# Column 0 of two folds on another engine, gathers ahead of angle rows, ten products moved into the last tiles, and transform copies put off

## The chip, the cores and the metric

The kernel runs on one core of one Trainium2 chip. A core has five engines that the text speaks of by their profile names: PE (TensorE, matrix products; its weight loads are PEld), DVE (VectorE), ACT (ScalarE), POOL (GpSimd) and SP (SyncE, which here only issues transfers). Each engine works through its own queue in order, and the engines wait for one another through semaphores, which are counters: an instruction names a counter and the value that it must have reached. The metric is the device time of one execution in microseconds (us); lower is better.

## The reference, cut to what matters

```python
X = np.fft.fft(x, axis=1)            # x: 8 batches x 3008 rows x 256 channels
X = np.fft.fft(X, axis=2)
x = X.real.reshape(8 * 3008, 256)
gate = np.maximum(x @ w_gate, 0.0)   # 256 -> 1536
val = x @ w_val
out = (gate * val) @ w_out           # 1536 -> 256, float32
```

So each batch gets a two-dimensional Fourier transform, of which the real part goes through a gated layer: two products with weight matrices, the relu of one times the other, and a third product.

## The kernel before, in words

**The transform.** The transform over the 256 channels is taken into the weights: TA and TB are cosine and sine matrices, and the kernel forms WA (cosine times weight) and WB (sine times weight) for gate and value. What is left is the transform over the 3008 rows. By symmetry it is folded: a row is added to, or subtracted from, its mirror row, in two halves of the batch (r = 0, 1) and three tiles of 128 row pairs (t = 0, 1, 2). XD holds rows read upward, XG the mirror rows read downward. Their sum goes to AA, and from AA the cosine inputs F and the sine inputs G are formed, 128 channels each. Products of F and G with tables of cosines and sines (`tabC`, `tabS`) then give the transform, U and V, whose columns are output rows.

**The start (batch 0).** For row tile 0 the mirror rows are loaded upward and turned by a product with a reversed identity (`turn`, L347). For row tiles 1 and 2 GpSimd issues four indirect gathers (`load_mirror`, L118), between small row fills: `iota` (L224) writes the index and angle rows, among them `urow`, of which two columns per row tile feed the angle products (`angle`, L313 and L314) that make the odd tables on ScalarE. After that GpSimd issues the first weight loads (`load_w`, L295), finishes TA and TB (L361, L363), and issues the other four weight loads and that of `w_out` (L367). On VectorE a loop over t folds: for t = 0 and each half, L422 writes channels 1 to 255 of AA, L423 channel 0 (which is stored twice, at 0 and at 256), then F (L391 for half 0, L389 for half 1), a small difference `hy` for channel 128 (L397), and G (L405). For t = 1 and 2 one L411 writes channels 1 to 255 of both halves, L412 channel 0, and then come F for both halves, `hy` and G for both halves. ScalarE turns `hy` into `ny` (L401). `dft_first` takes the products (L575, in the loop order half, then parity of the row pair) into four banks, with the weight products (L589) and angle products of later tables between them; ScalarE copies one bank out (L545, `es`), and VectorE forms sum and difference (L555) into U and V.

**The tiles.** The output is worked in blocks of columns, and each block in 12 tiles of 128 of the 1536 inner features. Batch 0 has four blocks of 376 or 377 columns, the others three blocks of 512, 512 and 481. A tile of batch 0 (`single_tile`) has on TensorE the gate (L816, L817), the mirror of the tile before (L822), the value (L816, L817) and the mirror of the gate (L822); ScalarE takes the relu (L832), and VectorE the product h (L841) for the column and its mirror. In later batches (`slot`) the gate is split over ScalarE, VectorE (L967) and GpSimd (L968), and VectorE forms h twice in a tile (L852). The output products with `w_out` (L729) of the block before are spread between these, some per tile; 24 of them, two groups of 12, fill a bank, which ScalarE copies (L742) and SP sends out (L752).

**The transform of the next batch** is a list of steps (`dft_steps`, L538) that batch 0 takes after its tiles, as many as the table `DFT_0` says. When a bank is complete, `end` puts its copy (L545, list `evict`) and its sums (L555, list `sums`) on two lists; in batch 0 `flush` issues both at once, and `run`, which a tile calls for output products, flushes too. The channel-128 rows are made in one step of this list (`nyquist_steps`), with two copies (L663).

**The end.** In the last block 8 output products per tile are taken (96 in 12 tiles). When the last tile's mirror and h are done, the block's own 96 output products follow without other work. SP moves the h columns that do not fill a group of 128 rows to a buffer LB (L847), which the last-but-one group reads.

The order on each queue is that in which the Python code issues the instructions; the tile framework adds the waits between engines from what each instruction reads and writes.

Of the kernel before, what the change touches and what calls it, by code (L numbers as in the profile page):

```python
# [15 lines left out]
ALU = mybir.AluOpType  # L16
# [18 lines left out]
def kernel(  # L35
# [8 lines left out]
    nc = tc.nc  # L44
    B, S, D = x.shape
# [177 lines left out]
    def iota(dst, pattern, base, mult):  # L223
        nc.gpsimd.iota(dst, pattern=pattern, base=base, channel_multiplier=mult, allow_small_or_imprecise_dtypes=True)  # L224
# [60 lines left out]
    iota(back[:], [[0, 1]], 127, -1)  # L285
    iota(gidx[:].rearrange("p (t r) -> p t r", r=2), [[-128, 3], [-H // 2, 2]], H - 1, -1)
    load_mirror(0, 1, 0)
    for t in (1, 2):
        iota(urow[0:1, 2 * t:2 * t + 2], [[1, 2], [2, 128]], 256 * t + 1, 0)
    nc.gpsimd.memset(urow[0:1, 5, 120:121], 0.0)  # L290
    load_mirror(0, 1, 1)
    hold(slice(2, 3))

    def load_w(i, c):
        nc.gpsimd.dma_start(out=wr[i][c], in_=(moe_w_gate, moe_w_val)[i][:, c * 512:(c + 1) * 512].rearrange("(c p) f -> p c f", p=128))  # L295
    for r in range(2):
        load_mirror(0, 2, r)
    load_w(0, 0)
    load_w(1, 0)
    nc.gpsimd.memset(sgn[:], 1.0)  # L300
# [60 lines left out]
    nc.gpsimd.tensor_scalar(TB[:, 0, 0:1], ad[:, 128:129], scalar1=-1.0 / 128, op0=ALU.mult, scalar2=0.5, op1=ALU.add)  # L361
    for T in (TA, TB):
        nc.gpsimd.tensor_tensor(T[:, 1, :], T[:, 0, :], sgn[:], op=ALU.mult)  # L363
    for c in (1, 2):
        for i in range(2):
            load_w(i, c)
    nc.gpsimd.dma_start(out=wo[:], in_=moe_w_out.rearrange("(c p) d -> p c d", p=128))  # L367
# [39 lines left out]
    for t in range(3):  # L407
        n = ROWS[1][t]
        p = slice(0, n)
        if t:  # L410
            nc.vector.tensor_tensor(AA[p, :, t, :, 1:D], XG[p, :, t, ::-1, 1:D], XD[p, :, t, :, D - 1:0:-1], op=ALU.add)  # L411
            nc.vector.tensor_tensor(AA[p, :, t, :, 0:D + 1:D], XG[p, :, t, ::-1, 0].unsqueeze(3).to_broadcast([n, 2, 2, 2]),  # L412
                                    XD[p, :, t, :, 0].unsqueeze(3).to_broadcast([n, 2, 2, 2]), op=ALU.add)
            for r in range(2):
                channels(p, r, t)
            half_128(p, t)
            for r in range(2):
                channels_g(p, r, t)
        else:
            nc.vector.memset(GG[1][:].rearrange("p i t q d -> p (i t q) d")[:, :, 0:1], 0.0)  # L420
            for r in range(2):
                nc.vector.tensor_tensor(AA[p, r, t, :, 1:D], upright[r][:, ::-1, 1:D], XD[p, r, t, :, D - 1:0:-1], op=ALU.add)  # L422
                nc.vector.tensor_tensor(AA[p, r, t, :, 0:D + 1:D], upright[r][:, ::-1, 0].unsqueeze(2).to_broadcast([n, 2, 2]),  # L423
                                        XD[p, r, t, :, 0].unsqueeze(2).to_broadcast([n, 2, 2]), op=ALU.add)
                channels(p, r, t)
                if r:
                    half_128(p, t)
                channels_g(p, r, t)
# [80 lines left out]
            return dst[:, 0:NJ], dst[:, NJ:2 * NJ]  # L509
        return dst[:, 3 * NJ:4 * NJ + 1], dst[:, 2 * NJ:3 * NJ]  # L510

    evict, sums = [], []

    def flush():
        for todo in (evict, sums):
# [3 lines left out]
    def family(b, dst, fam, sine, now=True, pool=None):  # L519

        n, cols = (NE, slice(0, NE)) if fam == 0 else (NJ, slice(NE, NK))
        src, tab = (GG[b % 2], tabS) if sine else (FF[b % 2], tabC)
        st, apart = {}, now or pool is not None

        def mm(par, t, nyq=False):
            if par not in st and not apart and not par:
                st[0] = st[1]
            elif par not in st:  # L530
                home, tag = pool or ((psG, "g") if now and not par else (psD, "d"))
                st[par] = home.tile([128, 512], F32, name=tag, tag=tag)
            rows = slice(0, ROWS[par][t])
            if nyq:
                nc.tensor.matmul(st[par][0:1, 0:n], lhsT=FF[b % 2][rows, fam, t, par, 128:129], rhs=tabC[rows, 2 * t + par, cols],
                                 start=False, stop=(t == 2), skip_group_check=True)
            else:
                nc.tensor.matmul(st[par][:, 0:n], lhsT=src[rows, 1 - fam if sine else fam, t, par, 0:128],  # L538
                                 rhs=tab[rows, 2 * t + par, cols], start=(t == 0 and (apart or par == 1)), stop=(t == 2),
                                 skip_group_check=not apart)  # L540

        def end(par):
            if par:
                st["es"] = rp.tile([128, NE], F32, name="es", tag="es", bufs=2)
                evict.insert(0, lambda: nc.scalar.copy(st["es"][:, 0:n], st[1][:, 0:n]))  # L545
            elif not apart:
                whole, rest_ = half_of(dst, fam)
                evict.insert(0, lambda: nc.scalar.copy(whole, st[1][:, 0:n]))
                for c in (slice(0, NJ // 2), slice(NJ // 2, NJ)):
                    sums.append(lambda c=c: nc.vector.scalar_tensor_tensor(rest_[:, c], in0=st["es"][:, c], scalar=2.0, in1=st[1][:, c],  # L550
                                                                           op0=ALU.mult, op1=ALU.subtract))
            else:
                for d, op in zip(half_of(dst, fam), (ALU.add, ALU.subtract)):
                    m = d.shape[-1]
                    sums.append(lambda d=d, op=op, m=m: nc.vector.tensor_tensor(d, st["es"][:, 0:m], st[0][:, 0:m], op=op))  # L555
            if now:
                flush()

        def at(par):
            home, tag = pool  # L560
            st[par] = home.tile([128, 512], F32, name=tag, tag=tag)
            return st[par]
        return mm, end, at

    def dft_first(U, V):
# [3 lines left out]

        def products(t, k, rs):  # L570
            src, tab = ((FF[1], tabC), (GG[1], tabS))[k]
            for r in rs:
                for par in (1, 0):
                    rows = slice(0, ROWS[par][t])
                    nc.tensor.matmul(bank[k, par][:, 0:NJ], lhsT=src[rows, r, t, par, 0:128], rhs=tab[rows, 2 * t + par, odd_k],  # L575
                                     start=(t == 0 and r == 0), stop=(t == 2 and r == 1), skip_group_check=bool(k))

        def nyquist(t):
            for par in (1, 0):
# [213 lines left out]
    def run(todo, n):  # L793
        for _ in range(min(n, len(todo))):
            todo.pop(0)()
        if not paired:
            flush()

    def run_one(todo):
# [213 lines left out]
    for b in range(B):  # L1013
# [4 lines left out]
        for blk, block in enumerate(blocks):  # L1018
# [39 lines left out]
            if (b, blk) == (0, 0):  # L1058
                for fi in range(NF):
                    st = tile_of(block, fi, (U, V, CB))  # L1060
                    add_h(st, hs)
                    if fi == 8:
                        todo_out = out_steps(b, block, hs, True)
                    pending = first_tile(st, more.get((0, fi), ()), 6)
                mirror(pending["g"], pending, 0)
                relu(pending)
            elif not paired:
                for fi in range(NF):
                    st = tile_of(block, fi, (U, V, CB))
                    add_h(st, hs)  # L1070
                    tag = {(3, 8): "g", (3, 9): "d", (3, 10): "g", (3, 11): "d"}.get((blk, fi), "p")
                    last = []
                    if (blk, fi) == (3, 11):
                        last = [lambda: (sine_part(ahead[1]), cosine_part(ahead[1]), both(ahead[1]), seed(ahead[2]))]
                    if (blk, fi) == (3, 9):
                        ahead = [next(tiles) for _ in range(3)]
                        more[(3, 9)] = [lambda: seed(ahead[0], prime())]
                        more[(3, 10)] = [lambda: seed(ahead[1], prime())]
                        more[(3, 11)] = [lambda: (sine_part(ahead[0]), cosine_part(ahead[0]), both(ahead[0]))]
                    if (blk, fi) == (1, 8):  # L1080
                        run(todo_out, len(todo_out))
                        todo_out = out_steps(b, block, hs, True)
                    pending = single_tile(st, 3 if blk == 1 else per_tile // 2, more_b.get((blk, fi), ()), last, tag)
                    run(todo_dft, DFT_0[blk - 1][fi])
            else:
                for fi in range(NF):
                    at = NF * blk + fi
                    cur = ahead.pop(0)
                    add_h(cur, hs)
                    ahead.append(next(tiles, None))  # L1090
                    pending = slot(cur, *ahead, per_tile, .72)
                    run(todo_dft, DFT_ODD[at] if b % 2 else DFT_EVEN[at])
            if b or blk > 1:
                run(todo_out, len(todo_out))
            if blk == len(blocks) - 1 or (b, blk) == (0, 1):
                run(todo_dft, len(todo_dft))
            if b or blk > 1:
                todo_out = out_steps(b, block, hs)
        if b:
            run_fold(99)  # L1100
# [34 lines left out]
```

## Time and profile before

| what | us |
|---|---|
| median of three runs | 634.59 (634.58 to 634.65) |
| the profiled execution | 634.97 |
| its span, first to last instruction | 633.2 |
| PE busy in the span | 620.3 (98%) |
| DVE busy | 553.8 (87%) |
| POOL busy | 507.0 (80%) |
| ACT busy | 446.8 (71%) |
| first gather issued, last gather issued (POOL L118) | 3.03, 8.19 |
| folds on DVE, first L422 to the end of the last L405 | 7.02 to 17.08 |
| batch 0's own transform products, last group begins (PE L575) | 17.67 |
| first tile's first product (PE, line 905) | 18.76 |
| last block's own output products begin (PE L729) | 618.72 |

Times of instructions are counted from the span's start. The 1.77 us between the span and the execution's time lie around the span. A matmul's duration holds its way through the array, so matmuls in a row start closer together than they last: 512 columns 0.2 us apart, 256 columns 0.11 us.

### The profile page before, as it was taken

The page shows a single profiled execution, that of the slowest core. Times are in us where ns is not written, and L with a number is a line of the kernel's source. Part 1 is how long each engine was busy: PE and PEld are TensorE (multiplying, and loading weights), DVE is VectorE, ACT ScalarE, POOL GpSimd, SP SyncE. Part 2 cuts the span into 40 slices and gives each one's busy share as a digit, 9 for nine tenths or more (in the row PEclk, how much of TensorE's full clock was granted, in tenths as well). Part 3 has the DMA queues.
Part 4 walks back from the last instruction along what each step waited for, and adds up shares of the span by engine and source line. Part 5 has one row for each costly group of instructions (what it writes and reads, how often), then busy time and mean ns, then how long its engine had stood idle before and what let it go on. Part 6 is the DMA issues. An engine that isn't in the chain of part 4 may idle for free.

```text
span 633.2 us, 12459 instructions
## 1 busy us (share of the span) xinstructions
PE 620.3 (98%) x4090; PEld 399.1 (63%) x4137; DVE 553.8 (87%) x983; ACT 446.8 (71%) x811; POOL 507.0 (80%) x495
## 2 busy tenths in 40 slices
PE   8999999999999999999999999999999999999997
PEld 2566666566666666666666666666666666666666
DVE  8896576998999899898999999898999989999991
ACT  6786667777777767777677767777777777777752
POOL 8988992998989998898879989699886656666660
PEclk9999999999999999999999999999999999999999
DMA  9953753714282427314272425311221111211122
GB/s 239 208 195 129 176 180 94 193 51 146 84 198 91 133 69 180 116 49 147 76 197 80 128 76 119 74 56 42 69 61 36 42 59 56 59 38 48 52 59 84
DMA packets 64196, 66.32 MB, mean 105 GB/s; under 512 B 19802, under 2 KB 47226, under 8 KB 64131
## 3 DMA queue, kind: packets, MB, share of 16 engines
q1 hardware_dynamic: 59715, 59.96, 33.0%
q0 software_dynamic: 3984, 4.92, 3.9%
q8 instruction: 32, 0.52, 0.4%
q10 hardware_dynamic: 432, 0.66, 0.3%
q14 instruction: 33, 0.27, 0.1%
HBM read 41.77 MB, written 34.13 MB: 120 GB/s over the span
## 4 chain that ended last, share of the span: by engine, by line
PE 88%; DVE 5%; DMA 2%; issue 2%; ACT 1%; POOL 1%; SPq 0%; DVEq 0%; ACTq 0%; POOLq 0%
PE o L729 35%; PE v L817 10%; PE v L822 10%; PE g L956 8%; PE p L963 8%; PE v L816 7%; PE d L538 4%; DVE h L852 3%; DMA xr<-in_x_dram 2%; PE p L822 1%; PE p L816 1%; PE p L817 1%; DVE r L967 1%; DMA XG<-in_x_dram,gidx 1%; DVE h L841 1%
## 5 line engine op out<-in xcount | busy, mean ns | idle before, releaser
L968 POOL TENSOR_TENSOR r<-r 128x512 f32<-128x512 f32 (+1 forms) x252 | 314.2, 1252 | 100.3 <-DVE r L967 99.9
L852 DVE SCALAR_TENSOR_TENSOR h<-r,v 128x512 bf16<-128x512 f32 (+1 forms) x504 | 318.7, 674 | 40.2 <-PE v L822 28.7
L729 PE MATMUL o<-wo,h 128*128 128x256 bf16 x2172 | 330.8, 272 | 0.0
L729 PEld LDWEIGHTS <-h 128*128 128x128 bf16 x2220 | 216.8, 98 | 113.3 <-issue 1.8
L951 ACT ACTIVATE p<-CB,b 128x512 f32<-128x512 bf16 (+1 forms) x252 | 172.4, 684 | 73.2 <-DVE r L967 71.5
L959 ACT COPY r<-g 128x512 f32<-128x512 f32 (+1 forms) x252 | 145.3, 577 | 67.6 <-PE g L956 58.1
L967 DVE SCALAR_TENSOR_TENSOR r<-r,p 128x512 f32<-128x512 f32 (+1 forms) x252 | 169.0, 671 | 0.6 <-ACT r L959 0.6
L817 PE MATMUL v<-V,WB 128*128 128x512 bf16 (+3 forms) x296 | 108.6, 367 | 2.3
L822 PE MATMUL v<-V,WM 128*128 128x512 bf16 (+1 forms) x252 | 94.4, 374 | 1.8 <-DVE h L852 1.1
L956 PE MATMUL g<-V,WM 128*128 128x512 bf16 (+1 forms) x252 | 94.5, 375 | 0.4 <-ACT r L959 0.3
L963 PE MATMUL p<-U,WA 128*128 128x512 bf16 (+1 forms) x252 | 94.5, 375 | 0.0
L816 PE MATMUL v<-U,WA 128*128 128x512 bf16 (+3 forms) x252 | 91.9, 365 | 0.0
L841 DVE TENSOR_TENSOR h<-r,v 128x376 bf16<-128x376 f32 (+1 forms) x88 | 45.1, 543 | 18.7 <-PE v L822 11.8
L816 PEld LDWEIGHTS <-WA 128*128 128x128 bf16 x347 | 33.8, 97 | 40.7 <-issue 12.1
L742 ACT COPY os<-o 128x512 f32<-128x512 f32 x92 | 52.5, 572 | 4.7 <-issue 4.1
L817 PEld LDWEIGHTS <-WB 128*128 128x128 bf16 x347 | 33.8, 97 | 34.1 <-DVE WB L381 0.6
L151 POOL TENSOR_TENSOR XG<-XG,XD 128x510 f32<-128x510 f32 x42 | 53.0, 1269 | 0.0
L832 ACT ACTIVATE r<-p 128x376 f32<-128x376 f32 (+1 forms) x80 | 38.3, 485 | 18.8 <-PE p L822 9.6
L159 POOL TENSOR_TENSOR AA<-XG 128x510 f32<-128x510 f32 x42 | 45.3, 1088 | 0.0
L956 PEld LDWEIGHTS <-WM 128*128 128x128 bf16 x252 | 24.6, 98 | 6.4 <-issue 1.0
L963 PEld LDWEIGHTS <-WA 128*128 128x128 bf16 x252 | 24.7, 98 | 3.4 <-issue 0.5
L822 PEld LDWEIGHTS <-WM 128*128 128x128 bf16 x252 | 24.6, 98 | 2.8
(177 smaller groups left out, 417.2 us busy)
## 6 DMA issues: line engine op xcount, KB each, us to landing
out_dram<-os SPq DMA_DIRECT2D x124, 128.0 KB
xr<-in_x_dram SPq DMA_DIRECT2D x12, 768.0 KB
XG<-xr SPq DMA_DIRECT2D x12, 768.0 KB
XD<-in_x_dram SPq DMA_DIRECT2D x15, 512.0 KB
out_dram<-os SPq DMA_DIRECT2D x35, 112.0 KB
XD<-in_x_dram SPq DMA_DIRECT2D x8, 448.0 KB
CB<-ch SPq DMA_DIRECT2D x7, 376.2 KB
out_dram<-os SPq DMA_DIRECT2D x13, 96.0 KB
```

The costliest lines, as they stand in the source:

```text
L151: e.tensor_tensor(XG[p, r, t, ::-1, 1:D], XG[p, r, t, ::-1, 1:D], XD[p, r, t, :, D - 1:0:-1], op=ALU.add)
L729: nc.tensor.matmul(st["p"][0:m, q, :], lhsT=lhs(f), rhs=wo[:, f, :], start=(f == 0 and not (early and q)), stop=(f == NF - 1), skip_group_ ...
L816: nc.tensor.matmul(bank[:, 0:st["n"]], lhsT=WA[i][:, st["f"]], rhs=st["us"], start=True, stop=False)
L817: nc.tensor.matmul(bank[:, 0:st["n"]], lhsT=WB[i][:, st["f"]], rhs=st["vs"], start=False, stop=True)
L822: nc.tensor.matmul(bank[:, 0:st["n"]], lhsT=W[i][:, st["f"]], rhs=v, start=False, stop=True, skip_group_check=True)
L852: nc.vector.scalar_tensor_tensor(half_h(st, sign), in0=st["s"][1 + sign][:, 0:n], scalar=0.0, in1=st["v"][:, 0:n], op0=ALU.max, op1=ALU.mult)
L951: nc.scalar.activation(st["p"][:, 0:st["n"]], st["c"], ACTF.Copy, scale=b2[:, st["fi"]:st["fi"] + 1])
L956: nc.tensor.matmul(st["g"][:, 0:n], lhsT=WM[0][:, st["f"]], rhs=st["vs"], start=True, stop=True)
L959: nc.scalar.copy(q[:, 0:n], st["g"][:, 0:n])
L963: nc.tensor.matmul(st["p"][:, 0:n], lhsT=WA[0][:, st["f"]], rhs=st["us"], start=False, stop=True, skip_group_check=True)
L967: nc.vector.scalar_tensor_tensor(sp[:, 0:n], in0=q[:, 0:n], scalar=-0.5, in1=st["p"][:, 0:n], op0=ALU.mult, op1=ALU.add)
L968: nc.gpsimd.tensor_tensor(sm[:, 0:n], sp[:, 0:n], q[:, 0:n], op=ALU.add)
```

## The change

Five edits, all in the order or place of work; no value that is computed changes.

- GpSimd's fill of `urow` for row tile 2 (one `iota` and a one-element memset) goes behind the four gathers; that of row tile 1 stays between the first and the second.
- Column 0 of row tiles 1 and 2 (before: L412 on VectorE) becomes `channel_0` on GpSimd. It is issued ahead of the weight loads of chunk 1 (row tile 1) and of chunk 2 (row tile 2), behind TA and TB.
- In `dft_first` the products of row tile 2 run parity first, then half.
- In batch 0, steps of the transform that `DFT_0` places 1 to 3 at a time, in any tile but the block's last, no longer flush: a flag `put_off` leaves copies and sums on their lists until the next tile's first group of output products.
- In the last block the last three tiles take 10, 10 and 14 output products in place of 8 each; the ten added ones are the first of the block's own group (tiles 0 to 9). They leave 86 for the end.

```diff
     load_mirror(0, 1, 0)
-    for t in (1, 2):
-        iota(urow[0:1, 2 * t:2 * t + 2], [[1, 2], [2, 128]], 256 * t + 1, 0)
-    nc.gpsimd.memset(urow[0:1, 5, 120:121], 0.0)
+    iota(urow[0:1, 2:4], [[1, 2], [2, 128]], 257, 0)
     load_mirror(0, 1, 1)
...
     for r in range(2):
         load_mirror(0, 2, r)
+    iota(urow[0:1, 4:6], [[1, 2], [2, 128]], 513, 0)
+    nc.gpsimd.memset(urow[0:1, 5, 120:121], 0.0)
     load_w(0, 0)
     load_w(1, 0)
...
+    def channel_0(t):
+        n = ROWS[1][t]
+        p = slice(0, n)
+        nc.gpsimd.tensor_tensor(AA[p, :, t, :, 0:D + 1:D], XG[p, :, t, ::-1, 0].unsqueeze(3).to_broadcast([n, 2, 2, 2]),
+                                XD[p, :, t, :, 0].unsqueeze(3).to_broadcast([n, 2, 2, 2]), op=ALU.add)
+
     for c in (1, 2):
+        channel_0(c)
         for i in range(2):
             load_w(i, c)
...
             nc.vector.tensor_tensor(AA[p, :, t, :, 1:D], XG[p, :, t, ::-1, 1:D], XD[p, :, t, :, D - 1:0:-1], op=ALU.add)
-            nc.vector.tensor_tensor(AA[p, :, t, :, 0:D + 1:D], XG[p, :, t, ::-1, 0].unsqueeze(3).to_broadcast([n, 2, 2, 2]),
-                                    XD[p, :, t, :, 0].unsqueeze(3).to_broadcast([n, 2, 2, 2]), op=ALU.add)
...
-            if now:
+            if now and not put_off:
                 flush()
...
-            for r in rs:
-                for par in (1, 0):
+            for r, par in [(r, par) for r in rs for par in (1, 0)] if t < 2 else [(r, par) for par in (1, 0) for r in rs]:
...
-        if not paired:
+        if not (paired or put_off):
             flush()
...
+                    put_off = 0 < DFT_0[blk - 1][fi] < 4 and fi < NF - 1
                     run(todo_dft, DFT_0[blk - 1][fi])
+                    put_off = False
...
-                    pending = slot(cur, *ahead, per_tile, .72)
+                    outs = per_tile
+                    if (b, blk) == (B - 1, 2) and fi > 8:
+                        outs = (10, 10, 14)[fi - 9]
+                        if fi == 9:
+                            rest = out_steps(b, block, hs)
+                            todo_out += rest[:10]
+                            del rest[:10]
+                    pending = slot(cur, *ahead, outs, .72)
...
-            if b or blk > 1:
+            if (b, blk) == (B - 1, 2):
+                todo_out = rest
+            elif b or blk > 1:
                 todo_out = out_steps(b, block, hs)
```

Line numbers below are those of the kernel before unless a line is said to be of the changed kernel, where they are up to 15 higher.

More of the change, by code (lines that the diff above doesn't have):

```diff
@@ L510, in half_of @@
         return dst[:, 3 * NJ:4 * NJ + 1], dst[:, 2 * NJ:3 * NJ]
-    evict, sums = [], []
+    evict, sums, put_off = [], [], False
     def flush():
@@ L571, in products @@
             src, tab = ((FF[1], tabC), (GG[1], tabS))[k]
-            for r in rs:
-                for par in (1, 0):
-                    rows = slice(0, ROWS[par][t])
-                    nc.tensor.matmul(bank[k, par][:, 0:NJ], lhsT=src[rows, r, t, par, 0:128], rhs=tab[rows, 2 * t + par, odd_k],
-                                     start=(t == 0 and r == 0), stop=(t == 2 and r == 1), skip_group_check=bool(k))
+            for r, par in [(r, par) for r in rs for par in (1, 0)] if t < 2 else [(r, par) for par in (1, 0) for r in rs]:
+                rows = slice(0, ROWS[par][t])
+                nc.tensor.matmul(bank[k, par][:, 0:NJ], lhsT=src[rows, r, t, par, 0:128], rhs=tab[rows, 2 * t + par, odd_k],
+                                 start=(t == 0 and r == 0), stop=(t == 2 and r == 1), skip_group_check=bool(k))
         def nyquist(t):
```

## The prediction

> **What bounds the kernel now.** I read the page first. Its section of busy times says that TensorE (PE) works nearly all the time, so a change gains only by closing one of its gaps, and loses whatever it makes TensorE wait.
>
> ```profile
> PE 620.3 (98%) x4090; PEld 399.1 (63%) x4137; DVE 553.8 (87%) x983; ACT 446.8 (71%) x811; POOL 507.0 (80%) x495
> ```
>
> The gaps are at the start, at a few places of batch 0 and at the end, which are the places that the change touches. So I read timelines there, engine by engine. (Columns: start, duration, engine, line, operation, idle time before it in brackets.) First the start, on VectorE (DVE), GpSimd (POOL) and TensorE:
>
> ```profile
> 8.60 0.68 DVE L422 TENSOR_TENSOR AA<-v,XD 128x510 f32<-128x510 f32 x1
> 11.52 0.43 DVE L412 TENSOR_TENSOR AA<-XG,XD 128x8 f32<-128x8 f32 x1
> 14.04 1.22 DVE L411 TENSOR_TENSOR AA<-XG,XD 121x1020 f32<-121x1020 f32 x1 [0.37 <-issue]
> 15.37 0.17 DVE L412 TENSOR_TENSOR AA<-XG,XD 121x8 f32<-121x8 f32 x1
> 15.57 0.43 DVE L391 TENSOR_TENSOR F<-AA 121x258 bf16<-121x258 f32 x1
> ...
> 11.89 0.42 POOL L363 TENSOR_TENSOR TB<-TB,sgn 128x128 bf16<-128x128 bf16 x1
> 12.26 0.78 POOL L295 DMA_DIRECT2D h<-in_moe_w_gate_dram  x1
> 13.03 0.73 POOL L295 DMA_DIRECT2D h<-in_moe_w_val_dram  x1
> ...
> 9.48 0.32 PE L314 MATMUL g<-q,minus 128*128 128x376 f16 x1
> 16.06 0.83 PE L575 MATMUL p<-tabC,F 121*128 121x376 bf16 x4 [0.22 <-DVE F L391]
> ```
>
> From 8.60 to 16.01 VectorE does one fold after another almost without rest; the fold of row tile 2 (15.57) releases TensorE at 16.06, and from there TensorE runs closely packed. Hence a delay of that fold goes into the end one to one. The only rest, 0.37 us before the L411 at 14.04, is called "issue". The view of that line shows four semaphore waits, the longest of 1431 ns, the last begun at 12.6. Taken as the same one it ends at 14.03: VectorE waited there for the last gather.
>
> ```profile
> L411 DVEq EVENT_SEMAPHORE  x4: 50/102/1431, 9.5 to 12.6; - x4
> ```
>
> Then batch 0 and the end:
>
> ```profile
> 58.88 1.00 DVE L555 TENSOR_TENSOR U<-es,g 128x377 bf16<-128x377 f32 x2 [0.38 <-PE g L538]
> 60.29 0.32 PE L816 MATMUL p<-U,WA 128*128 128x376 bf16 x1
> 60.85 0.32 PE L822 MATMUL v<-CB,WB 128*128 128x376 bf16 x1
> 72.50 0.32 PE L822 MATMUL p<-CB,WB 128*128 128x376 bf16 x1 [0.44 <-ACT r L832]
> ...
> 615.01 0.36 PE L822 MATMUL v<-V,WM 128*128 128x481 bf16 x1
> 616.76 0.36 PE L822 MATMUL v<-V,WM 128*128 128x481 bf16 x1
> 618.51 0.36 PE L822 MATMUL v<-V,WM 128*128 128x481 bf16 x1 [0.65 <-DVE h L852]
> 618.72 2.78 PE L729 MATMUL o<-wo,h 128*128 128x256 bf16 x24
> ```
>
> Sums of the transform on VectorE (58.88) push the products h back, and TensorE loses 0.24 us at 60.85; a copy on ScalarE costs it 0.59 us at 72.50; at the end it waits for h before 616.76 (0.26 us) and 618.51 (0.81 us), with 96 output products still to do.
>
> **The change part by part.** *Start, gathers.* One angle row (L224, 0.49 us) and a memset go behind the gathers, so gathers two to four are issued about 0.6 us sooner; the two weight loads behind them stay at 9.2 us. That would remove the 0.37 us wait. It only counts if VectorE gets there in time.
>
> *Start, column 0.* L412 leaves VectorE: 0.46 us (11.52 to 11.98) and 0.20 us (15.37 to 15.57). Where it went matters more. In the changed program's list of waits, this VectorE instruction has a new one:
>
> ```
> L422 TensorTensor AA<-v,XD 128x2x255 [waits DMAHW2,PE]        before
> L427 TensorTensor AA<-v,XD 128x2x255 [waits DMAHW2,PE,Pool]   after
> ```
>
> It is the second L422, the fold of half 1 of row tile 0, at 8.60 us before. Its count is 20, and the instruction that raises GpSimd's count to 20 is the second `channel_0`, that of row tile 2. (Both write AA; a box around `channel_0`'s strided write, from half 0 to half 1, contains what L422 writes.) So VectorE, which works in order, stops in the middle of row tile 0, with all folds of row tiles 1 and 2 queued behind, until GpSimd has done row tile 2's column 0; and on GpSimd that comes behind the weight issues of chunks 0 and 1.
>
> When is that? TB's product ends at 11.89 + 0.42 = 12.31, plus about 0.05 for the moved rows: 12.36. `channel_0` handles 8 elements a row; the nearest GpSimd rows are L201 (6 elements, 212 ns) and L183 (12 elements, 234 ns), so 0.22, with 0.05 for a wait: 12.63. (Ends: 0.11, the memset at L302, and 0.43, what L412 took on VectorE; 0.2 us either way.) Two weight issues, 0.77 + 0.72 start to start: 14.1. The second `channel_0` has four wait instructions before it at about 0.06 (L412 at 15.37 began 0.10 after L411's end, with one) and 0.22 of work: 14.57. Its gathers have landed by then. VectorE resumes at 14.62, not 8.60.
>
> From there to row tile 2's fold it needed 15.57 - 8.60 = 6.97 us. Out of that go 0.46 and 0.20 (L412), 0.37 (the gather is there), and 0.19 by which the L391 beside TB's product was stretched (11.98 to 12.52 against 15.57 to 15.92): 5.75. The fold starts at 20.37: **4.8 us late**.
>
> TensorE and ScalarE add to it. ScalarE has row tile 0's small copy (L401, 10.65) ahead of its last two angle chains; it waits for the same fold, until 16.06, and the last chain also needs a TensorE product that now comes at 17.3. Its rows to the next L401 (12.13 to 13.50, 1.37 us) end at 19.1 with their start at 17.7; the product with it, the four sine products and the four weight products (0.41 + 0.65 + 0.86, spacing at 13.75 to 15.84) put L575's first at 21.27, against 16.06: **5.2 us** instead of 4.8.
>
> That is at full speed. But TensorE now rests from 9.80 to 16.0. The nearest rows are those after its first rest, which lasted to 1.20 us:
>
> ```profile
> 6.36 0.52 PE L313 MATMUL g<-krow,urow 95*128 95x376 f16 x1
> 6.67 0.52 PE L314 MATMUL g<-q,minus 128*128 128x376 f16 x1
> ...
> 8.36 0.33 PE L313 MATMUL d<-krow,urow 95*128 95x376 f16 x1
> 8.52 0.32 PE L314 MATMUL d<-q,minus 128*128 128x376 f16 x1
> ```
>
> Products of 376 columns came 0.31 us apart, and 0.16 apart from 8.36 on; of the four turn passes (L347) the last, from 7.8, took 0.68 us, the others 1.06 to 1.19. So the fast pace came at about 7.8, 5.3 us after the first table product at 2.48. If TensorE restarts slowly at 16.0 and is fast again at 21.3, the angle product ends at 18.5 instead of 17.6, the chain's copy at 20.3, and L575 starts at 22.7: **6.65 us**. Ends: nothing more (5.2), and slow up to L575 itself (23.9, so 7.8). I take 6.65, since a rest of 6.2 us is nearer to that start than to the 0.85 us rest ahead of 12.65, after which the pace was still 0.16.
>
> [...]
>
> *Row tile 2's new order.* The first bank is complete after two products instead of three, so V is there 0.16 earlier; L907 started 0.12 after its place: **-0.1**.
>
> *Copies put off.* Two products h now precede the sums (L555). In block 1's tile 11 they run at 59.43 and 59.89, the sums from 60.35 to 61.35. But the second sum is the stretch of U that block 2's first gate reads, and in the program that L816 waits for it: 61.4 instead of 60.29. The 0.24 at 60.85 then vanishes: **+0.87**. (Ends: -0.24 and +1.1.) In block 3 the same stall (0.24 at 95.95) goes without that harm: -0.24. At 72.50 the relu comes first, but the next transform product needs the bank that the two copies (0.95) leave, at 71.87 + 0.95 + 0.05 = 72.87, where it started at 72.88: 0. Two stalls of 0.09 at 77.33 and 82.26 may close: -0.2. Together **+0.45**.
>
> *Ten products.* Tiles 9 to 11 take 10, 12 and 6 products between the mirrors instead of 8, 8 and 3. At 0.109 each the mirrors at 615.01, 616.76 and 618.51 come at 615.12, 617.04 and 618.79; then 86 products end at 618.79 + 0.21 + 9.38 = 628.38 against 618.72 + 10.47 = 629.19: **-0.8**. h of tiles 0 to 9 is long there.
>
> Sum: 6.65 - 0.1 + 0.45 - 0.8 = **+6.2 us**. The profiled execution took 634.97 (span 633.2 and 1.77 around it), 0.38 above the median, so I add to the median: 634.59 + 6.2 = 640.8.
>
> **The rivals.** *TensorE keeps its pace over the rest.* For it: no row shows a slow spell after 8.36. Against: no rest was over 0.9 us. 5.2 - 0.1 + 0.45 - 0.8 = +4.75: 639.3.
>
> *The new wait is not binding (not slower).* Place: the second L422. If the count that it needs were reached before 8.60 us, as by an earlier GpSimd instruction, the head would be near nothing: row tile 1's folds wait for the first `channel_0` until 12.7 instead of 11.98, and the 0.37 and the second L412 give that back (20.37's counterpart is 15.5). Then 0 - 0.1 + 0.45 - 0.8: 634.1. It decides if GpSimd's twentieth count comes before 9 us; against it stands that nothing ahead of `channel_0` counts so far.
>
> *Slow longer.* TensorE stays slow through L575 and the stage after it, +7.8 and more: 642 to 643.
>
> **How the numbers follow.** Forecast 0.62, full pace 0.24, slow longer 0.10, not binding 0.04. What the measurement can tell from no change is about 0.2%, 1.3 us. The range 638.8 to 642.4 takes in both paces with 0.2 for `channel_0` and 0.5 for the sums. Slower by over 0.2%: the first three, 0.96 less a little for what I mis-saw, 0.95; same 0.03; faster 0.02.
>
> **What would show it.** In the changed profile: VectorE idle about 6 us before the second L427, released by POOL; TensorE idle from about 9.8 to 16; 376-column products 0.31 apart after 16; L579's last group of `p` near 22.7 (21.3 at full pace); the L820 that opens block 2 waiting about 1 us for the U sums; the last block of products 10 fewer and ending about 0.8 nearer its mirror. Wrong would be a second L427 near 8.6, or a later stage that gives the delay back.

## The result, and the profile after

The changed kernel takes 641.27 us (median of five runs, 641.25 to 641.72), the kernel before 634.59 (five runs beside it, 634.45 to 634.78): 1.0107 times as long, 95% interval 1.0092 to 1.0121, or 6.7 us more. The profiled execution took 641.27 us with a span of 639.5, so 1.77 lie around it, as before. Line numbers are those of the changed kernel from here on.

The busy times on the page have hardly moved; TensorE has the same 4090 products on record in a longer span:

```profile
PE 622.1 (97%) x4090; PEld 400.0 (63%) x4137; DVE 552.2 (86%) x981; ACT 447.2 (70%) x811; POOL 506.9 (79%) x497
```

The timeline of the start (columns: start, duration, engine, line, operation, idle time before it and what ended it):

```profile
11.98 0.21 POOL L367 TENSOR_TENSOR AA<-XG,XD 128x8 f32<-128x8 f32 x1
12.12 0.78 POOL L293 DMA_DIRECT2D h<-in_moe_w_gate_dram  x1
12.90 0.73 POOL L293 DMA_DIRECT2D h<-in_moe_w_val_dram  x1
14.26 0.20 POOL L367 TENSOR_TENSOR AA<-XG,XD 121x8 f32<-121x8 f32 x1 [0.63 <-issue]
...
14.49 0.69 DVE L427 TENSOR_TENSOR AA<-v,XD 128x510 f32<-128x510 f32 x1 [6.00 <-POOL AA L367]
20.08 0.43 DVE L398 TENSOR_TENSOR F<-AA 121x258 bf16<-121x258 f32 x1
...
15.90 0.81 PE L579 MATMUL p<-tabC,F 128*128 128x376 bf16 x2 [5.33 <-DVE F L396]
17.98 0.50 PE L313 MATMUL d<-krow,urow 95*128 95x376 f16 x1
18.27 0.52 PE L314 MATMUL d<-q,minus 128*128 128x376 f16 x1
22.39 0.81 PE L579 MATMUL p<-tabC,F 121*128 121x376 bf16 x4
```

VectorE's second L427, the fold of half 1 of row tile 0, stands still for 6.00 us until GpSimd's second `channel_0` (14.26) is done. GpSimd itself was through with its weight issues at 13.63; the 0.63 us of rest ahead of 14.26 are a semaphore wait for row tile 2's last gather, whose last part landed at 14.04. The longest of `channel_0`'s waits, of 1645 ns, begun at 12.43, ends at 14.07 (columns: count, shortest, median and longest in ns, first and last start):

```profile
L367 POOLq EVENT_SEMAPHORE  x5: 17/42/1645, 11.3 to 14.1; - x5
```

So row tile 0's fold has come to wait, by way of GpSimd, for the last gather of row tile 2. In the seven traces with this wait the gather landed at 13.69 to 14.16, the second `channel_0` began 0.22 later, and the fold another 0.23 later, each time. The fold of row tile 2 comes at 20.08 instead of 15.57 (+4.51), and TensorE's last group of p at 22.39 instead of 16.06 (+6.33). The two angle products at 17.98 and 18.27 are 0.29 apart; at full pace it is 0.16, as from 8.36 on in the kernel before. The stretches of the start show why (columns: stretch, length, busy time and count on PE, PEld, DVE, ACT, POOL, then granted TensorE clock, DMA share and GB/s):

```profile
10.00:12.00 2.00, 0.57 (x4) 0.13 (x2) 0.00 (x0) 0.97 (x2) 1.94 (x8) 1.00 1.07 202
12.00:14.00 2.00, 0.00 (x0) 0.00 (x0) 0.00 (x0) 0.00 (x0) 1.63 (x4) 0.76 1.14 214
14.00:16.00 2.00, 0.10 (x1) 0.10 (x2) 1.44 (x5) 0.05 (x1) 1.51 (x3) 0.50 1.23 202
16.00:18.00 2.00, 2.00 (x7) 0.39 (x7) 1.97 (x4) 1.50 (x4) 1.86 (x6) 0.50 1.24 205
18.00:20.00 2.00, 2.00 (x7) 0.71 (x6) 2.00 (x5) 1.14 (x3) 0.00 (x0) 0.53 1.22 201
20.00:22.00 2.00, 1.56 (x10) 0.72 (x10) 1.63 (x9) 0.62 (x3) 0.33 (x4) 1.00 1.37 197
```

While TensorE rests, its granted clock falls to half, and it stays there for the first four microseconds of work. By the trace's record of the clock it falls at 13.05 us and is back at 19.88.

From there I followed the distance between the two kernels, product by product. It is 6.33 us at the last group of p, 6.19 from the first tile's second gate product on (L907 at 19.47 before, L911 at 25.66 in the changed kernel), 7.42 after block 2's first gate, 7.79 after one stall that the kernel before does not have, 7.34 at the end of block 3, 7.37 where the last block's three changed tiles begin, and 6.56 at the last product. At that second gate product of the first tile, which needs V, the kernel before lost 0.12 us and the changed one nothing; first the rows before, then those of the changed kernel:

```profile
18.92 0.59 PE L377 MATMUL o<-h,TA 128*128 128x512 bf16 x2
19.47 0.32 PE L907 MATMUL p<-V,WB 128*128 128x376 bf16 x1
```

```profile
25.23 0.59 PE L384 MATMUL o<-h,TA 128*128 128x512 bf16 x2
25.66 0.32 PE L911 MATMUL p<-V,WB 128*128 128x376 bf16 x1
```

The rows on TensorE at block 2's first gate, and at a mirror seven microseconds later:

```profile
67.95 0.32 PE L820 MATMUL p<-U,WA 128*128 128x376 bf16 x1 [0.94 <-DVE U L560]
74.96 0.32 PE L826 MATMUL v<-CB,WB 128*128 128x376 bf16 x1 [0.25 <-DVE h L845]
```

The first is the expected wait for the U sums (60.29 and no wait before). The second is the stall that nobody expected; TensorE is 0.36 us later behind it than ahead of it.

### The profile page after: what moved, and what is told of

It is laid out like the page before. It is cut to its first block, busy times and chain, and to the rows that moved or that the text cites. A ratio compares the mean times of both kernels' runs of the same rounds, so it can differ in the third digit from the quotient of the medians.

```text
span 639.5 us, 12460 instructions
## 1 busy us (share of the span) xinstructions
PE 622.1 (97%) x4090; PEld 400.0 (63%) x4137; DVE 552.2 (86%) x981; ACT 447.2 (70%) x811; POOL 506.9 (79%) x497
## 4 chain that ended last, share of the span: by engine, by line
PE 90%; DVE 4%; issue 2%; ACT 1%; DMA 1%; POOL 1%; DVEq 0%; POOLq 0%; ACTq 0%
PE o L733 35%; PE v L821 10%; PE v L826 10%; PE g L960 8%; PE p L967 8%; PE v L820 7%; PE d L543 4%; DVE h L856 3%; PE p L826 1%; DMA XG<-in_x_dram,gidx 1%; PE p L820 1%; PE p L821 1%; DVE r L971 1%; PE d L661 1%; POOL XG L118 1%
```

## The experiments

All ratios are to the kernel before, on the same chip, by runs made side by side.

### Column 0 back on VectorE

```diff
-        nc.gpsimd.tensor_tensor(AA[p, :, t, :, 0:D + 1:D], XG[p, :, t, ::-1, 0].unsqueeze(3).to_broadcast([n, 2, 2, 2]),
+        nc.vector.tensor_tensor(AA[p, :, t, :, 0:D + 1:D], XG[p, :, t, ::-1, 0].unsqueeze(3).to_broadcast([n, 2, 2, 2]),
...
     for c in (1, 2):
-        channel_0(c)
...
             nc.vector.tensor_tensor(AA[p, :, t, :, 1:D], XG[p, :, t, ::-1, 1:D], XD[p, :, t, :, D - 1:0:-1], op=ALU.add)
+            channel_0(t)
```

> The changed kernel with one edit taken back: column 0 of row tiles 1 and 2 is on VectorE again; the order of the gathers, the put-off copies and the ten products stay changed. My theory: the whole start delay (6.33 us at the first value product) hangs on column 0 being on GpSimd, so 641.3 - 6.3 = about 635.0, and VectorE's second L427 is back near 8.6. What is left against the kernel before is +0.4: about +1.0 from the put-off copies and +0.2 to +0.4 unexplained in block 0, less 0.8 from the ten products. Rival: a good part of the delay comes from the moved angle rows and gathers (the angle product of row tile 2 waits for its row, the gathers crowd the other loads): then it stays above 637.

Measured: 634.62 us, ratio 1.0001 (0.9992 to 1.0010). VectorE's second L427 is back:

```profile
8.85 0.69 DVE L427 TENSOR_TENSOR AA<-v,XD 128x510 f32<-128x510 f32 x1 [0.35 <-issue]
13.87 1.22 DVE L417 TENSOR_TENSOR AA<-XG,XD 121x1020 f32<-121x1020 f32 x1
15.39 0.43 DVE L397 TENSOR_TENSOR F<-AA 121x258 bf16<-121x258 f32 x1
```

It came lower than expected (635.0), within what the measurement can tell. The 6.33 that the expectation puts at the first value product is the distance at the last group of p. So the whole loss goes with this one edit, and the other four together are worth nothing that shows. Product by product, this kernel is 0.14 us ahead of the kernel before after the start, 0.28 behind at the eighth tile of block 1, 1.14 behind after block 2's first gate, 0.71 behind at the end of block 3; the tail gives that back. Against this kernel the changed one is 6.32 us late at the first tile, 6.28 before and 6.63 after the stall at 74.96.

### Column 0 on GpSimd, issued behind its own fold

The same GpSimd and VectorE instructions in the same order on both engines, but each `channel_0` is written in the program behind the L418 of its row tile:

```diff
-    for c in (1, 2):
-        channel_0(c)
-        for i in range(2):
-            load_w(i, c)
-    nc.gpsimd.dma_start(out=wo[:], in_=moe_w_out.rearrange("(c p) d -> p c d", p=128))
...
             nc.vector.tensor_tensor(AA[p, :, t, :, 1:D], XG[p, :, t, ::-1, 1:D], XD[p, :, t, :, D - 1:0:-1], op=ALU.add)
+            channel_0(t)
+            for i in range(2):
+                load_w(i, t)
+            if t == 2:
+                nc.gpsimd.dma_start(out=wo[:], in_=moe_w_out.rearrange("(c p) d -> p c d", p=128))
```

> The changed kernel, column 0 still on GpSimd with the same instructions in the same order on every engine; only the place in the program is another: each of the two is issued behind the fold of channels 1 to 255 of its own row tile instead of ahead of all folds, so that the tile framework makes GpSimd wait for VectorE's fold, and VectorE only in front of F of the same row tile. My theory: the delay comes from the order in which the overlapping write boxes are issued, not from GpSimd's work. F of row tile 1 then waits for GpSimd until about 12.7 (11.98 before), F of row tile 2 comes near 15.7 (15.57 before), TensorE has no long rest and keeps its pace, and the time is 635.0 (634.6 to 635.6). Rival: GpSimd is simply too late with column 0 behind its weight loads and the fold of row tile 2 still waits for it: then 638 to 641.

Measured: 635.95 us (635.09 to 637.0), ratio 1.0021 (1.0011 to 1.0032). On VectorE:

```profile
9.04 0.69 DVE L427 TENSOR_TENSOR AA<-v,XD 128x510 f32<-128x510 f32 x1 [0.55 <-issue]
12.96 0.43 DVE L393 TENSOR_TENSOR F<-AA 128x258 bf16<-128x258 f32 x1 [1.03 <-POOL AA L367]
15.92 0.43 DVE L393 TENSOR_TENSOR F<-AA 121x258 bf16<-121x258 f32 x1 [0.33 <-POOL AA L367]
```

The 6 us wait is gone though GpSimd does the same work. What made it was the place in the program: issued ahead of row tile 0's second fold, `channel_0` becomes something that this fold must wait for. That a box around its write is the reason is argued from what the two instructions write; no run changed the write alone. The rival (GpSimd is too late with the work itself) falls, but the edit is no gain either, and the time is 0.35 us above the upper end that I gave. The trace, of the slowest of the eight runs (637.00), says where time went there. GpSimd now waits for VectorE, 1.31 us at the second `channel_0`, and behind it in GpSimd's queue stand the last two weight loads and that of `w_out`. TensorE waits for the last of these, and for GpSimd's work behind them:

```profile
21.03 0.32 PE L826 MATMUL p<-CB,WB 128*128 128x376 bf16 x1 [0.22 <-POOL CB L489]
32.71 0.49 PE L733 MATMUL o<-wo,h 128*128 128x256 bf16 x3 [0.90 <-DMA wo<-in_moe_w_out_dram]
```

Another 0.36 us goes at the mirror at 70.70, by the same stall as in the changed kernel at 74.96, which a later run explains.

### TensorE kept busy over its rest

```diff
         angle(4, 5)
+        busy = psD.tile([128, 512], F32, name="d", tag="d")
+        for _ in range(24):
+            nc.tensor.matmul(busy[:], lhsT=warm[:, 0:128], rhs=warm[:], start=True, stop=True)
         products(0, 0, (1,))
```

> The changed kernel with 24 more products of 512 columns on TensorE (of zeros, into a bank that the next product overwrites), between the angle product at 10.25 and the first product that waits for VectorE at 15.9, so that TensorE does not rest there. My theory: TensorE is late by 4.5 us because of VectorE, and the other 1.8 us of the 6.33 come from the slow restart and the ScalarE chain behind it; without the rest the products from 15.9 run 0.16 apart, the last group L579 of p starts near 21.0 instead of 22.39, and the time is about 1.1 to 1.4 less: 640.0 (639.7 to 640.3). Rival: the wide spacing after the rest is not due to the rest (the weights, ScalarE, or loads slow the products): then the time stays at 641.3 or, if the added products are in the way, above.

Measured: 639.92 us (639.86 to 640.1), ratio 1.0084 (1.0070 to 1.0098), 1.35 below the changed kernel.

```profile
9.98 5.34 PE L608 MATMUL d<-warm 128*128 128x512 bf16 x24 [0.35 <-ACT a L318]
15.84 0.49 PE L579 MATMUL p<-tabC,F 128*128 128x376 bf16 x2 [0.52 <-DVE F L396]
17.08 0.33 PE L313 MATMUL d<-krow,urow 95*128 95x376 f16 x1
17.25 0.32 PE L314 MATMUL d<-q,minus 128*128 128x376 f16 x1
21.18 0.81 PE L579 MATMUL p<-tabC,F 121*128 121x376 bf16 x4
```

VectorE is as late as in the changed kernel (its second L427 starts at 14.44), and TensorE starts again at the same time, but at full pace; the last group of p comes at 21.18, 1.21 sooner. More work on TensorE makes the kernel faster, so the pace after the rest, and not the work, cost these 1.2 to 1.4 us.

### Half of that

The same with 12 added products, so that TensorE rests 3.12 us (12.73 to 15.85).

> As the run with TensorE kept busy, but with 12 added products instead of 24: they end near 13, so TensorE rests some 2.8 us ahead of 15.9 instead of 5.3 (changed kernel) or 0.5 (24 added). [...]

Measured: 641.51 us (641.09 to 642.12), ratio 1.0105 (1.0090 to 1.0121): no better than no added product (641.27). On TensorE:

```profile
15.85 0.49 PE L579 MATMUL p<-tabC,F 128*128 128x376 bf16 x2 [3.12 <-DVE F L396]
17.09 0.33 PE L313 MATMUL d<-krow,urow 95*128 95x376 f16 x1
17.26 0.32 PE L314 MATMUL d<-q,minus 128*128 128x376 f16 x1
17.85 1.40 PE L579 MATMUL p<-tabC,F 128*128 128x376 bf16 x4 [0.27 <-DVE F L398]
19.98 1.44 PE L579 MATMUL o<-tabS,G 128*128 128x376 bf16 x4
22.14 0.81 PE L579 MATMUL p<-tabC,F 121*128 121x376 bf16 x4
```

and by stretches:

```profile
14.00:16.00 2.00, 0.15 (x1) 0.11 (x2) 1.49 (x5) 0.10 (x1) 1.56 (x3) 1.00 1.24 203
16.00:18.00 2.00, 1.73 (x9) 0.42 (x8) 1.97 (x4) 1.83 (x5) 1.81 (x6) 0.98 1.24 204
18.00:20.00 2.00, 1.99 (x7) 0.37 (x6) 2.00 (x5) 1.18 (x4) 0.00 (x0) 0.50 1.25 202
20.00:22.00 2.00, 2.00 (x9) 0.97 (x9) 1.59 (x9) 0.30 (x2) 0.37 (x4) 0.67 1.36 195
```

TensorE starts at full pace, works so for two microseconds, and its clock is halved then, in the middle of its work, from 17.92 to 21.34. The clock answers to the rest, since without it (24 products, mean granted clock 1.000 in all five runs) it stays full, but 2.07 us after the rest is over.

### Nothing put off

```diff
-                    put_off = 0 < DFT_0[blk - 1][fi] < 4 and fi < NF - 1
+                    put_off = False
```

> The changed kernel with the flag for putting off copies and sums always false; all else as changed. My theory: block 2's first gate gets its U sums in time again (-0.87), the stall near the b copy of block 2 (0.36), seen only in the changed kernel, goes with it, and block 3's stall of 0.24 comes back: 641.27 - 0.99 = 640.3. Rival 1: the stall of 0.36 has nothing to do with the put-off copies (it follows from the late start): 640.6. Rival 2: the waits are taken back later in batch 0, since ScalarE and VectorE catch up: 641.2, no difference.

Measured: 640.66 us (640.22 to 641.14), ratio 1.0098 (1.0083 to 1.0114): rival 1. Product by product against the changed kernel, and less what its start was ahead (0.25; the last gather landed at 13.79 instead of 14.04), it gains 0.38 at the eighth tile of block 1, 0.86 more at block 2's first gate, and gives 0.42 back up to the end of block 3; together 0.82. The stall with h is there unchanged:

```profile
73.46 0.32 PE L826 MATMUL v<-CB,WB 128*128 128x376 bf16 x1 [0.25 <-DVE h L845]
```

### All put off but the step ahead of block 2

```diff
-                    put_off = 0 < DFT_0[blk - 1][fi] < 4 and fi < NF - 1
+                    put_off = 0 < DFT_0[blk - 1][fi] < 4 and fi < NF - 1 and (blk, fi) != (1, 10)
```

> The changed kernel, but the copies and sums of block 1's eleventh tile (those ahead of block 2) are not put off; all other put-off places stay. My theory: only this place costs: the 0.87 of block 2's first gate goes, and block 3's gain stays: 641.27 - 0.87 = 640.4, or 640.0 if the 0.36 stall near the b copy of block 2 follows from it as well. Rival: the put-off copies of block 2's own tiles (one step at a time, between bank and sums) make the 0.36 stall: 640.4 with that stall still there near 74.1.

Measured: 639.83 us (639.6 to 641.45), ratio 1.0079 (1.0065 to 1.0092). By the traces this place is worth 0.80 us (0.87 in the sum), and the stall with h is gone as well (another 0.36). The profiled execution was the longest, 641.45 us: its TensorE clock stayed at half until 24.02, and its start is 1.66 later than that of the changed kernel.

So the same stall stays where nothing is put off and goes where one step less is put off. The two runs together fit neither theory. What the kernels with the stall have in common is a number: how many instructions stand on VectorE ahead of that h.

### One more instruction on VectorE

```diff
+    nc.vector.memset(single("extra", [1, 1])[:], 0.0)
     for t in range(3):
         n = ROWS[1][t]
```

> The changed kernel with one more instruction on VectorE: a fill of one element, 0.06 us, before the first fold, where VectorE rests 6 us soon after. Nothing else changes but the number that every later VectorE instruction has in its queue. In the traces so far the row 192 on VectorE (semaphore waits counted) begins 0.40 us after the wait ahead of it ended, in every kernel where a wait stands just before it, and rows 64, 448, 1088, 1216 and 1472 do the same: steps of 128. In the changed kernel row 192 is the h that holds TensorE at 74.96. If the lapse belongs to the number, the wait ahead of that h takes row 192 now, the h begins 0.06 after its wait, TensorE's stall of 0.36 is gone, and the time is 640.9. Rival: the lapse belongs to this h (to the relu that it waits for, or to a transfer at that time): then the stall stays and the time is 641.3.

Measured: 640.67 us (640.45 to 640.81), ratio 1.0089 (1.0075 to 1.0103), 0.60 below the changed kernel for 0.06 us more work. Of this the trace puts 0.35 on the stall, which is gone, and 0.22 on an earlier start (the last gather landed at 13.69 instead of 14.04). The rows on VectorE, first of the changed kernel, then of this one:

```profile
72.59 0.16 DVE L786 TENSOR_SCALAR b<-d 128x12 f32<-128x12 f32 x1
73.91 1.00 DVE L845 TENSOR_TENSOR h<-r,v 128x376 bf16<-128x376 f32 x2 [1.15 <-ACT r L836]
```

```profile
72.37 0.16 DVE L787 TENSOR_SCALAR b<-d 128x12 f32<-128x12 f32 x1
73.33 1.00 DVE L846 TENSOR_TENSOR h<-r,v 128x376 bf16<-128x376 f32 x2 [0.79 <-PE v L827]
```

With the waits counted as rows of VectorE's queue (numbers from 1, read off the trace):

```
changed:   191 wait for the mirror, ends 73.51   192 h, starts 73.91   (0.40 later)
one more:  192 wait for the mirror, ends 73.29   193 h, starts 73.33   (0.05 later)
```

The relu named in the first profile row was only what had happened last. The lapse belongs to the number.

### The ten products taken back

```diff
-                        outs = (10, 10, 14)[fi - 9]
-                            todo_out += rest[:10]
-                            del rest[:10]
```

> The changed kernel with 8, 8 and 8 output products in the last three tiles and all 96 of the block's own at the end. My theory: the ten products fill the waits of TensorE for h before the last two mirrors (0.26 and 0.81), so without them +0.8: 642.1 (641.9 to 642.3). Rival: the end is set by the last copies and stores and not by TensorE: below 641.6.

Measured: 642.25 us (641.74 to 642.86), ratio 1.0116 (1.0101 to 1.0132). Its profiled execution starts 0.42 later than that of the changed kernel, is 0.50 behind at the mirror before the changed tiles and 1.31 at the last product: 0.81 for the ten products.

### The gathers alone

```diff
-    for t in (1, 2):
-        iota(urow[0:1, 2 * t:2 * t + 2], [[1, 2], [2, 128]], 256 * t + 1, 0)
-    nc.gpsimd.memset(urow[0:1, 5, 120:121], 0.0)
+    iota(urow[0:1, 2:4], [[1, 2], [2, 128]], 257, 0)
...
         load_mirror(0, 2, r)
+    iota(urow[0:1, 4:6], [[1, 2], [2, 128]], 513, 0)
+    nc.gpsimd.memset(urow[0:1, 5, 120:121], 0.0)
```

(in the kernel before)

> The kernel before with one edit alone: the fill of row tile 2's angle row and its one-element memset go behind the four gathers. The prediction's step: the last gather is issued 0.6 us sooner and lands sooner, so that the 0.37 us rest of VectorE ahead of the fold of row tile 2 goes: 634.2. Rival, which the trace of the changed kernel speaks for (issued at 7.60, landed about 14.1, as late as before): the landing is set by what the transfers share, not by the issue, so 634.6, and the rest of VectorE stays within 0.1 of 0.37.

Measured: 634.71 us, ratio 0.9998 (0.9989 to 1.0007).

```profile
14.17 1.22 DVE L411 TENSOR_TENSOR AA<-XG,XD 121x1020 f32<-121x1020 f32 x1 [0.18 <-issue]
```

The last gather is issued at 7.59 instead of 8.19 and lands at 14.09 instead of 13.96, and the fold that needs it starts at 14.17 instead of 14.04. The rest before it is shorter (0.18 against 0.37) only because VectorE came later: its second fold of row tile 0 started at 8.91 in this execution and at 8.60 in that of before. My bound for the rest, within 0.1 of 0.37, was missed; the time was not.

### The two parts that pay

The kernel before with the ten products and with copies put off in block 3 alone.

```diff
+                    put_off = 0 < DFT_0[blk - 1][fi] < 4 and fi < NF - 1 and blk == 3
...
+                        outs = (10, 10, 14)[fi - 9]
```

> The kernel before with the ten products moved, and copies put off in block 3 alone; the start and blocks 1 and 2 as before. Sum by the steps that the traces bear out: -0.8 for the ten products and -0.24 for block 3's stall, so 633.55 (633.3 to 633.9), faster than both kernels. Rival: a stall taken away in block 3 comes back at the next wait of batch 0, so -0.8 alone: 633.8.

Measured: 633.61 us (633.24 to 633.71), ratio 0.9981 (0.9972 to 0.9990), 1.1 below the 634.70 of the kernel before beside it: the theory, and less time than either kernel. Against the kernel before it is 0.28 ahead from block 3 on and 1.11 ahead at the last product. On TensorE at the end:

```profile
618.50 0.36 PE L822 MATMUL v<-V,WM 128*128 128x481 bf16 x1 [0.33 <-DVE h L852]
618.70 1.69 PE L729 MATMUL o<-wo,h 128*128 128x256 bf16 x14
```

It was 0.65 us of waiting ahead of that mirror before; half of it holds products now, and 14 instead of 24 are left in that bank.

## Why the prediction was right, and where its steps were not

640.8 was forecast, 641.27 measured. The likeliest case came, by its own mechanism. Part of the closeness is luck: by the traces the start cost 0.36 us less than in the sum and the put-off copies 0.37 more, which cancel, and a stall of 0.36 that was not in the sum is most of what is left.

- **The new wait.** Place and releaser were right: VectorE's second fold waits for GpSimd's second `channel_0`. VectorE resumed at 14.49 (predicted 14.62), and the fold of row tile 2 came at 20.08 (20.37), so 4.5 late instead of 4.8. That size came out by luck. The sum took `channel_0` to start when two weight issues were through, at 14.1, with its gathers landed by then. The issues were through at 13.63, and the gather, which landed at 14.04, set the time. That the place in the program makes the wait, and not the work on GpSimd, is shown by the run that only moved it; the box remains argued.
- **ScalarE and the products behind it at full pace.** 21.27 was predicted; with TensorE kept busy the group came at 21.18, though the fold of row tile 2 came at 20.02 there, 0.35 sooner than in the sum.
- **The slow restart.** Predicted 1.45 us (6.65 - 5.2), measured 1.35 in time and 1.21 at that group. The failed figure is the moment of recovery: 21.3 predicted from the first start, 19.88 measured, 4.0 us after the restart instead of 5.3. That moment differs from execution to execution: without the ten products it was 21.27, and the group of p came at 22.81 there, 6.75 late, near the 6.65 of the sum. By the clock record the clock is at half (0.50) for 6.83 us, from 13.05 to 19.88. With 12 added products, where the rest was 3.12 us, it was full at the restart (1.00 from 14 to 16 us) and went to half 2.07 us after it, from 17.92 to 21.34.
- **The gathers.** The step "the 0.37 us wait goes, because the gathers are issued 0.6 sooner" failed. In the changed kernel GpSimd itself waited for the last one until about 14.1, as long as VectorE had before (14.0); with the gathers alone the fold was no earlier either. Issued at 8.19 the last gather landed at 13.96 and 13.98 (two traces), issued at 7.6 at 13.63 to 14.16 (ten). The share of the DMA engines' time is above 1 from 4 us on (1.04 to 1.37 in stretches of two microseconds up to 22 in the changed kernel), so the landing is probably set by what the transfers share; that was not tried by itself.
- **Row tile 2's new order.** -0.1 predicted, -0.12 measured: the first tile's second gate product comes 0.59 us after its first in all nine traces with the new order, 0.71 in the three with the old one. ScalarE's copy for V starts 0.16 sooner, counted from the last group of o.
- **Copies put off.** +0.87 at block 2's first gate (0.80 and 0.86 measured in two comparisons) and -0.24 in block 3 (-0.24 and -0.28 measured) were right, and so was nothing at the copies of the channel-128 rows. Missed was the first place, block 1's sixth tile: two tiles later TensorE waits 0.24 us for a relu, and 0.38 are lost in all. The part is +0.82 instead of +0.45.
- **Ten products.** -0.8 predicted, -0.81 measured, three times.
- **What was not in the sum.** +0.36 for the h at 74.96. Two instructions and a wait left VectorE's queue, and so another instruction took row 192. This belongs to the removal of L412 as much as the 0.66 us that were counted.

The sum that the traces bear out: 6.33 - 0.14 + 0.82 + 0.36 - 0.81 = 6.56, which is how late the last product is (0.12 of the 0.14 is row tile 2's new order); the medians differ by 6.68. The forecast was 6.65 - 0.1 + 0.45 - 0.8 = 6.2.

## What to carry to other kernels

Before work is moved to an engine that is free, ask which instructions of the other engine come behind it in the program and write near what it writes, and what the moved work itself waits for. Here the framework ordered by the place of issue, and a wait in the middle of VectorE's queue held all that stood behind it until a transfer for a later row tile had landed. A rest that a change opens on TensorE can cost more than its length: here 1.2 to 1.4 us of slow time came behind 5.3 us of rest. And when a stall appears at an instruction that the change does not touch, count the instructions ahead of it on its queue before looking for a cause in its data: here a stall of 0.36 us was gone with one more instruction ahead of the h.

## What the runs showed of the hardware that was not expected

**Behind a wait, every 128th row of VectorE's queue starts 0.4 us late in these traces.** I took all rows of VectorE that stand right behind a wait row which ended when the engine was idle; there are some 200 in each of the twelve traces. They start 0.045 us after their wait (median), and at most two in a trace take more than 0.2. At the rows 64, 192, 320 and so on (steps of 128, waits counted) the same time is 0.395 to 0.402 us, without exception: rows 192, 1088 and 1216 of the changed kernel, 448 and 1472 of the kernel before, 960 with one more instruction. The DMA view of the changed kernel has this line (columns: packets, MB, share of 16 engines):

```profile
q14 instruction: 33, 0.27, 0.1%
```

In that trace a packet of this queue starts beside each of VectorE's 13 rows 64, 192 and so on to 1600, in ten cases within 1.2 us of the row and in the others up to 5.9 us after it. What holds the rows back was not shown. TensorE has no idle time behind row 192 where VectorE had work in hand (the kernel before, where VectorE was busy until 0.13 us ahead of that row) or was waiting anyway (the run with one more instruction, where that row is a wait and h starts 0.05 us behind it).

**The steps of TensorE's clock lie 3.41 us, or a multiple of it, apart in these traces.** By the clock record TensorE's clock went to half and back at 13.05 and 19.88 in the changed kernel, at 14.45 and 21.27 without the ten products, at 13.78 and 24.02 in the long execution with one put-off step less, at 17.92 and 21.34 with 12 added products: one, two or three times 3.41 us at half. The stretch at full clock between two steps fits as well: 621.23 us in the changed kernel is about 182 times 3.413. How long the half clock lasted shows in the run times. With 12 added products two runs had a mean granted clock of 0.997 and took 641.09 and 641.16 us; two had 0.994 and took 641.87 and 642.12. With one put-off step less the run at 0.991 took 641.45, the four at 0.994 and 0.995 took 639.6 to 639.9. The run that kept TensorE busy had 1.000 in all five and stayed within 0.24 us (639.86 to 640.1). Why the clock changes at another moment in each execution was not shown. Nor is the clock all of the scatter: the kernel before, at 0.999 to 1.000, went from 634.22 to 635.59 in 18 runs, and where VectorE waits for the last gather, its landing moved by 0.47 us from trace to trace.
